# Four y tiles, gathers behind scatters, weight splits behind the expert's tiles, and an even pace for the next route

## The chip, the cores and the metric

The kernel runs on one core of a Trainium2 chip. The metric is the device time of one execution in microseconds, lower is better. Five engines work side by side, each through its own instructions in order: TensorE (PE, with its weight loads as PEld), VectorE (DVE), ScalarE (ACT), GpSimd (POOL) and SyncE (SP). They wait for each other by semaphores.

## What is computed

The first part is an attention without softmax on 8 sequences of 2496 rows: `x = u * (relu(z zT / S)^2 v)`. The second part sends the 19968 rows of x through eight experts, 2496 rows each, chosen greedily:

```python
logits = x @ w_gate
order = np.argsort(-logits.flatten())
for idx in order:
    tok, e = (int(idx) // E, int(idx) % E)
    if assigned[tok] >= 0 or counts[e] >= cap:
        continue
    assigned[tok] = e
    counts[e] += 1
for e in range(E):
    mask = assigned == e
    h = np.maximum(x[mask] @ w1[e], 0.0)
    out[mask] = h @ w2[e]
```

## The kernel before

The attention takes the first 1503 us or so. `route(0)` then finds the first expert to be filled and its rows, with nothing else to do beside it. After that the experts follow each other, in the order in which they fill up.

An expert is 5 groups of rows (four of 512, one of 448) times 8 tiles of the hidden layer, so 40 steps (`PER`). The loop over n (L633) runs, in each step: `layer2` of step n (12 matmuls of 128x256 into the PSUM tiles y0 and y1, L545 to L547), the items of `todo` for n, `advance`, `layer1` of step n + 3 (6 matmuls into hp, L514 to L516, then hh by ScalarE L533 and hl by VectorE L534), and `advance` again. Every product is three matmuls, of high and low halves.

`todo` holds, for a group that begins at n0: `gather_x` at n0 - 12 (four indirect gathers on GpSimd into an xg tile, L446), `turn_x` at n0 - 6 and n0 - 5 (transposes on TensorE L499, xh on ScalarE, xl on VectorE), and `put_y` at n0 + 7 (two copies of y0 and y1 to a y tile by ScalarE L572, four indirect scatters by GpSimd L578). `split_w` turns a weight block into two halves, by ScalarE (L473, w1h and w2h) and VectorE (L475, w1l and w2l). For an expert that begins at step n0 it stands at n0 - 10 to n0 - 7 for the first half of the hidden layer (c = 0), at n0 - 4 to n0 - 1 for the second (c = 1).

`route(k + 1)` is a generator, worked off in pieces beside expert k by `advance`, twice a step (80 half steps). Each `yield` has a weight; the weights between two half steps must reach the half step's share of `YIELDS`, 88. A route closes the full expert, finds each row's best one again, then searches a threshold in two stages of several rounds. A round is: the mask (VectorE, L299), a histogram of it (TensorE, L230, 10 matmuls), hd, hr and hx (VectorE, L234 to L237), the sum over partitions by `onesr` (TensorE, L317), best, Dg and T (VectorE). At the end stand a count (fmask, L347), a prefix sum (`tri`, L382), and the list of the expert's rows: 156 matmuls in four parts (L431), each behind four tiles' quarters of ob on VectorE (L425), which gives idx. The last route has no search.

The order of an engine's instructions is set by the scheduler, which takes the program's order and its own estimate of when an operand is ready. `tc.issue_after(x)` orders an instruction behind x on x's own engine, and adds no semaphore.

Of the kernel before, what the change touches and what calls it, by code (L numbers as in the profile page):

```python
# [8 lines left out]
F32 = mybir.dt.float32  # L9
# [4 lines left out]
AF = mybir.ActivationFunctionType  # L14
# [81 lines left out]
def moe(tc, xd, first, jp, identf, w1, w2, out, B, S, cp):  # L96
    nc = tc.nc
    E, D, F = w1.shape
# [4 lines left out]
    DH = D // 128  # L103
    FT = F // 128
    J = B * NT + B // 2
# [12 lines left out]
    AHEAD = 12  # L118
    YIELDS = 88
    with ExitStack() as ctx:  # L120
# [104 lines left out]
        def hist(masks, n, order):  # L225
            p = srch()
            per = NC // len(masks)
            for c in range(NC):
                q, r = divmod(c, per)
                nc.tensor.matmul(p[:, :n * 16], oh[:, c * 16:(c + 1) * 16].rearrange("p j e -> p (j e)"),  # L230
                                 masks[q](slice(r * 16, (r + 1) * 16)), start=(c == 0), stop=(c == NC - 1))
            v = p[:, :n * 16]
            v = v.rearrange("p (t j) -> p t j", t=n) if order == "tj" else v.rearrange("p (j t) -> p t j", t=n)
            nc.vector.tensor_mul(hd[:, :n, :16], v, diag[:, None, :].to_broadcast([128, n, 16]))  # L234
            r = rp.tile([128, ND], F32, name="hr")
            nc.vector.tensor_reduce(r[:, :n], hd[:, :n], axis=AX.X, op=OP.add)
            nc.vector.tensor_mul(hx[:, :, :n], r[:, None, :n].to_broadcast([128, E, n]),  # L237
                                 dE[:, :, None].to_broadcast([128, E, n]))
            return hx, n + n % 2

        paced = []

        def behind(lag):
            return tc.issue_after(paced[-lag].ins) if len(paced) >= lag else nullcontext()

        def route(k):
            if k:
                closed = rp.tile([128, E], F32, name="closed", tag="rab")
                nc.vector.tensor_scalar(closed, ROUTE[k - 1]["star"], SHUT, None, op0=OP.mult)
                for c in range(0, JP, JP // 2):  # L250
                    o = lg[:, c:c + JP // 2]
                    nc.vector.tensor_add(o, o, closed[:, None, :].to_broadcast([128, JP // 2, E]))
                    yield 0.7
                for c in range(0, JP, JP // 4):
                    eq = rp.tile([128, JP // 4, E], BF, name="eq")
                    best_expert(nc, rp, first, slice(c, c + JP // 4), eq)
                    yield 6.8 / 4
                done = rp.tile([128, JP], F32, name="done")
                nc.vector.tensor_scalar(done, asg, 0.0, GONE, op0=OP.is_gt, op1=OP.mult)
                nc.vector.tensor_add(m, m, done)  # L260
                order_keys(nc, first, slice(0, JP))
                yield 1.5
            last = k == E - 1
# [12 lines left out]
            else:  # L276
# [7 lines left out]
                for stage in range(2):  # L284
                    V = floor
                    for r, w in enumerate(widths):
# [7 lines left out]
                        for h in range(nh):  # L294
# [6 lines left out]
                            mask.append(lambda j, t=t, n=n: t[:, j, :n])  # L301
                        yield 2
                        x, nn = hist(mask, n, "jt")
# [6 lines left out]
                        elif r + 1 < len(widths):  # L310
                            W = rp.tile([128, ND], F32, name="W", bufs=2)
                            n2 = (1 << widths[r + 1]) - 1
                            nc.vector.tensor_tensor(W[:, :n2], step[:, r + 1, :n2], V.to_broadcast([128, n2]), op=OP.add)
                        yield 2.2
                        p = srch()
                        o = p[:, :E * nn]
                        nc.tensor.matmul(o, onesr, x[:, :, :nn], start=True, stop=True)  # L317
                        best = rp.tile([128, E, ND], F32, name="best")
# [8 lines left out]
                    if stage == 0:  # L327
                        base = rp.tile([128, 1], F32, name="base")
                        nc.vector.tensor_scalar(base, tstar, 65536.0, None, op0=OP.mult)
                        rel = rp.tile([128, JP], F32, name="rel")  # L330
                        nc.vector.scalar_tensor_tensor(rel, first["top"], base, first["low"],
                                                       op0=OP.subtract, op1=OP.add)
                        near = rp.tile([128, JP], I16, name="near")
                        nc.vector.tensor_scalar(near, rel, 32767.0, -32768.0, op0=OP.min, op1=OP.max)
                        spread(nc, xr, near)
                        yield 1.5
                T = tstar
# [3 lines left out]
                take()  # L341
                yield
                x, nn = hist([lambda j: g[:, :, j]], 2, "tj")
                yield
                p = srch()
                o = p[:, :E * 2]
                nc.tensor.matmul(o, onesr, x[:, :, :2], start=True, stop=True)  # L347
                o = o.rearrange("p (e t) -> p e t", t=2)
# [26 lines left out]
            if not last:  # L375
# [3 lines left out]
                nc.vector.scalar_tensor_tensor(rem, star, FULL, rem, op0=OP.mult, op1=OP.add)  # L379
            yield 2.5  # L380
            p = srch()
            nc.tensor.matmul(p[:, :nl], tri, tot[:, :nl], start=True, stop=True)  # L382
            off = rp.tile([128, 2], F32, name="off")
# [20 lines left out]
            yield 2  # L404
            idx = rp.tile([128, KT], I32, name="idx", bufs=2)
            ROUTE[k]["idx"] = idx
            obs = {}
            for a0, a1 in ((0, 4), (4, KT)) if k == 0 and KT > 4 else ((0, KT),):
                na = a1 - a0
                p = srch()  # L410
                for c in range(0, JP, CB):
# [5 lines left out]
                    for i, d in enumerate((idh, idl)):  # L417
                        nc.vector.tensor_mul(hl[:, :, i], oa, by_quad(d[:, q], na))
                    yield 1.5
                    if a0 == 0:  # L420
                        obs[c] = rp.tile([128, QN, 128, QW], BF, name="ob", bufs=4)
                        for b in range(0, 128, 32):
                            z = b + 32
                            with behind(4):
                                nc.vector.tensor_tensor(obs[c][:, :, b:z], by_quad(rab[:, 1, q], z - b),  # L425
                                                        slot[:, None, b:z].to_broadcast([128, QN, z - b, QW]),
                                                        op=OP.is_equal)
                            yield 1.5
                    for j in range(c, min(J, c + CB)):
                        n, r = divmod(j - c, QW)  # L430
                        nc.tensor.matmul(p[:, :2 * na], obs[c][:, n, :, r], hl[:, n, :, :, r],  # L431
                                         start=(j == 0), stop=(j == J - 1))
                    yield
                idl_f = rp.tile([128, KT], F32, name="idl_f")[:, :na]
# [24 lines left out]
        def split_w(k, layer, c, half):  # L459
# [13 lines left out]
            nc.scalar.activation(h, src, AF.Copy)  # L473
            if k:
                nc.vector.tensor_sub(l, src, h.bitcast(F32))  # L475
            else:
                with tc.issue_after(paced[-1].ins if paced else ROUTE[0]["listed"].ins):
                    nc.vector.tensor_sub(l, src, h.bitcast(F32))

        def gather_x(k, g):  # L480
            t = fp.tile([128, 4, D], F32, name="xg")
            idx = ROUTE[k]["idx"]
            for i in range(4):
                n = min(128, S - 512 * g - 128 * i)
                gather(t[:n, i], xd, idx[:n, 4 * g + i:4 * g + i + 1])
            XG[k, g] = t
# [23 lines left out]
        def expand(k, g, f, p, c):  # L510
            for d in range(DH):
                wh, wl = [t[:, d, f % 4] for t in W1[k, f // 4]]
                xh, xl = XH[k, g, d][:, c], XL[k, g, d][:, c]
                nc.tensor.matmul(p[:, c], wh, xh, start=(d == 0), stop=False)  # L514
                nc.tensor.matmul(p[:, c], wh, xl, start=False, stop=False)  # L515
                nc.tensor.matmul(p[:, c], wl, xh, start=False, stop=(d == DH - 1))  # L516

        def layer1(k, g, f):
# [13 lines left out]
            l = fp.tile([128, 512], F32R, name="hl_", bufs=LA + 1)[:, :w]  # L532
            nc.scalar.activation(h, p, AF.Relu)  # L533
            paced.append(nc.vector.scalar_tensor_tensor(l, p, 0.0, h.bitcast(F32), op0=OP.max, op1=OP.subtract))  # L534
            HH[k, g, f], HL[k, g, f] = h, l

        def contract(k, g, f, i):
# [8 lines left out]
            nc.tensor.matmul(o, h[:, c], wl, start=False, stop=False, skip_group_check=True)  # L546
            nc.tensor.matmul(o, l[:, c], wh, start=False, stop=final, skip_group_check=True)  # L547

# [12 lines left out]
        def put_y(k, g):  # L561
            y = fp.tile([128, 4, D], F32, name="y")
            idx = ROUTE[k]["idx"]
# [53 lines left out]
        def advance(pos):  # L617
# [4 lines left out]
            if pos < skip:  # L622
                return
            want = -(-(pos % (2 * PER) - skip + 1) * YIELDS // (2 * PER - skip))
            if (pos + 1) % (2 * PER) == 0:
# [339 lines left out]
```

## Time and profile before

| | |
|---|---|
| timed runs, us | 2693.76, 2694.63, 2691.26 |
| median, us | 2693.76 |
| profiled execution, us | 2689.33 |
| its span, us | 2687.6 |
| mean granted TensorE clock | 0.979 |
| attention, first route, experts | to about 1503, to about 1594, to the end |

A row of waits reads: engine, tile and line that waited, what it waited for, us in total, times, longest. A row of a timeline: start, duration, engine, line, operation, out<-in, with the idle time before it and what ended that. A row of windows: stretch, its length, then busy time and instructions of PE, PEld, DVE, ACT and POOL, the granted clock, the share and rate of the DMA engines. A row of groups: line, engine, operation, names, shapes, count, busy us, mean ns, idle time before. The wait rows of two stretches (1677 to 1745 us, 1745 to 2690 us) stand in one block in the prediction, apart by a line of dots.

### The profile page before, as it was taken

How to read it: one execution, taken by the hardware profiler on the slowest of the kernel's cores; microseconds unless marked ns; L12 is line 12 of the kernel's file. 1: busy time of each engine (PE TensorE's matmuls, PEld its weight loads, DVE VectorE, ACT ScalarE, POOL GpSimd, SP SyncE). 2: the span in 40 equal slices, each digit the busy share in tenths (PEclk: the TensorE clock that was granted, in tenths of full speed). 3: DMA queues.
4: the chain of work that ended last, by engine and by line, in shares of the span. 5: the costliest groups of instructions: out<-in, count | busy, mean ns of one | idle time of the engine just before them, and what ended most of it. 6: DMA issues, size and time to landing. Idle time of an engine off the chain costs nothing.

```text
span 2687.6 us, 51810 instructions
## 1 busy us (share of the span) xinstructions
PE 2584.4 (96%) x19733; PEld 2415.5 (90%) x19733; DVE 1968.6 (73%) x6093; ACT 1649.3 (61%) x2867; POOL 362.1 (13%) x506
## 2 busy tenths in 40 slices
PE   8999999999999999999999759899999999999998
PEld 8999999999999999999999647888989898889997
DVE  7788887787787887887877777868586868686322
ACT  8888888898888888888888312323333323333332
POOL 3000000000000000000000003232333323333331
PEclk9999999999999999999999769999999999999999
DMA  4121220121211211211100011111121211121110
GB/s 140 37 73 39 60 73 30 49 71 35 67 53 33 79 47 49 66 32 52 47 32 9 15 40 47 63 42 68 39 70 38 71 38 68 42 81 57 43 46 23
DMA packets 51210, 138.88 MB, mean 52 GB/s; under 512 B 10641, under 2 KB 18321, under 8 KB 50065
## 3 DMA queue, kind: packets, MB, share of 16 engines
q1 hardware_dynamic: 35856, 94.66, 11.3%
q0 software_dynamic: 15104, 40.91, 4.8%
q8 instruction: 154, 2.52, 0.4%
q14 instruction: 96, 0.78, 0.1%
HBM read 85.47 MB, written 40.89 MB: 47 GB/s over the span
## 4 chain that ended last, share of the span: by engine, by line
PE 93%; DVE 4%; another core or an unknown queue 1%; DMA 1%; issue 1%; ACT 1%; POOL 0%; POOLq 0%; ACTq 0%; SPq 0%
PE acc L804 14%; PE acc L801 14%; PE acc L803 13%; PE sc L761 7%; PE sc L760 7%; PE y L545 5%; PE hp L514 5%; PE y L547 5%; PE y L546 5%; PE hp L516 5%; PE hp L515 5%; PE srch L230 2%; PE srch L431 2%; PE xp L499 1%
## 5 line engine op out<-in xcount | busy, mean ns | idle before, releaser
L804 PE MATMUL acc<-vl,hi 128*128 128x256 f32 x3200 | 896.2, 282 | 0.0
L801 PE MATMUL acc<-vh,hi 128*128 128x256 f32 x3200 | 892.6, 281 | 0.0
L803 PE MATMUL acc<-vh,lo 128*128 128x256 f32 x3040 | 853.1, 281 | 0.6 <-DVE lo L785 0.6
L785 DVE TENSOR_TENSOR lo<-a,hi 128x512 fp32r<-128x512 f32 (+1 forms) x760 | 512.4, 674 | 221.9 <-ACT hi L774 203.9
L801 PEld LDWEIGHTS acc<-vh,hi 128*128 128x128 f32 x3200 | 601.3, 188 | 28.6
L804 PEld LDWEIGHTS acc<-vl,hi 128*128 128x128 f32 x3200 | 601.5, 188 | 1.6
L803 PEld LDWEIGHTS acc<-vh,lo 128*128 128x128 f32 x3040 | 570.9, 188 | 31.9 <-DVE lo L785 1.0
L763 ACT ACTIVATE r<-sc 128x512 f32<-128x512 f32 (+1 forms) x800 | 467.8, 585 | 140.6 <-PE sc L761 135.7
L533 ACT ACTIVATE hh<-hp 128x512 fp32r<-128x512 f32 (+1 forms) x320 | 187.5, 586 | 582.8 <-PE hp L516 432.0
L768 ACT ACTIVATE a<-r 128x512 f32<-128x512 f32 (+1 forms) x800 | 497.1, 621 | 24.9 <-DVE lo L785 0.4
L831 DVE SCALAR_TENSOR_TENSOR lt<-xs,wgb 128x256 bf16<-128x256 f32 x1248 | 472.2, 417 | 0.3
L545 PE MATMUL y<-w2h,hh 128*128 128x256 f32 (+1 forms) x1280 | 367.6, 287 | 17.2 <-ACT y L572 13.3
L546 PE MATMUL y<-w2l,hh 128*128 128x256 f32 (+1 forms) x1280 | 363.4, 284 | 0.0
L760 PE MATMUL sc<-za 128*128 128x512 f32 (+1 forms) x800 | 316.0, 395 | 0.0
L761 PE MATMUL sc<-zb,za 128*128 128x512 f32 (+1 forms) x800 | 312.8, 391 | 0.0
L774 ACT ACTIVATE hi<-a 128x512 fp32r<-128x512 f32 (+1 forms) x480 | 298.3, 622 | 14.6
L545 PEld LDWEIGHTS y<-w2h,hh 128*128 128x128 f32 (+1 forms) x1280 | 241.7, 189 | 28.6 <-ACT y L572 15.2
L514 PE MATMUL hp<-xh,w1h 128*128 128x512 f32 (+2 forms) x646 | 264.2, 410 | 0.3 <-ACT xh L507 0.3
L515 PE MATMUL hp<-xl,w1h 128*128 128x512 f32 (+2 forms) x646 | 252.3, 391 | 0.0
L546 PEld LDWEIGHTS y<-w2l,hh 128*128 128x128 f32 (+1 forms) x1280 | 241.6, 189 | 10.8 <-issue 1.6
L516 PE MATMUL hp<-xh,w1l 128*128 128x512 f32 (+2 forms) x646 | 251.3, 390 | 0.0
L578 POOL DMA_INDIRECT out_dram<-y,idx x160 | 179.6, 1123 | 402.9 <-ACT y L572 356.5
(1139 smaller groups left out, 3418.0 us busy)
## 6 DMA issues: line engine op xcount, KB each, us to landing
vr<-in_v_dram SPq DMA_DIRECT2D x32, 512.0 KB, 3.6
ur<-in_u_dram SPq DMA_DIRECT2D x32, 512.0 KB, 4.4
xd<-xs SPq DMA_DIRECT2D x32, 512.0 KB, 2.9
wr<-in_moe_w_dram SPq DMA_DIRECT2D x32, 512.0 KB, 4.4
zb<-za SPq DMA_DIRECT2D x14, 640.0 KB, 6.8
zin<-in_z_dram SPq DMA_DIRECT2D x32, 128.0 KB, 2.1
vr<-in_v_dram SPq DMA_DIRECT2D x8, 384.0 KB, 3.3
ur<-in_u_dram SPq DMA_DIRECT2D x8, 384.0 KB, 4.4
```

The lines of the kernel that those rows point to most:

```text
L514: nc.tensor.matmul(p[:, c], wh, xh, start=(d == 0), stop=False)
L545: nc.tensor.matmul(o, h[:, c], wh, start=first, stop=False, skip_group_check=True)
L546: nc.tensor.matmul(o, h[:, c], wl, start=False, stop=False, skip_group_check=True)
L760: nc.tensor.matmul(p, k, ZA[b][:, q], start=True, stop=False)
L761: nc.tensor.matmul(p, k, ZB[b][:, q], start=False, stop=True)
L763: nc.scalar.activation(r, p, AF.Relu, scale=scale)
L768: nc.scalar.activation(a, R.pop(n), AF.Square)
L785: nc.vector.tensor_sub(l, a, h.bitcast(F32))
L801: nc.tensor.matmul(o, h[:, c], vh, start=(kt == 0 and i % 2 == 0), stop=False, skip_group_check=True)
L803: nc.tensor.matmul(o, l[:, c], vh, start=False, stop=False, skip_group_check=True)
L804: nc.tensor.matmul(o, h[:, c], vl, start=False, stop=last, skip_group_check=True)
L831: nc.vector.scalar_tensor_tensor(t[r], XS[b, g][r, i], 1.0, WG["rows"][r, e], op0=OP.mult, op1=OP.mult, accum_out=lg[r, j, e:e + 1])
```

## The change

It has five parts.

- The y tile has four buffers, where it had the pool's two.
- `gather_x` orders its four gathers behind the last scatter written so far, on GpSimd.
- `split_w` of every expert but the first orders its ScalarE copy behind the last hh, and its VectorE subtraction behind the last hl.
- The search's and the list's matmuls (`in_turn`) stand on TensorE behind the last matmul of layer 1 or 2 written so far.
- The weights of the yields are new and sum to about 79 of 80 half steps in place of about 103 against a ceiling of 88, so that no remainder is left for the last half step.

```diff
+        halves = []
+        layered = []
+        def in_turn():
+            return tc.issue_after(layered[-1].ins) if layered else nullcontext()
...
 # in hist; the same with in_turn() at L317, L347, L382 and L431
-            for c in range(NC):
-                q, r = divmod(c, per)
-                nc.tensor.matmul(p[:, :n * 16], ...)
+            with in_turn():
+                for c in range(NC):
+                    q, r = divmod(c, per)
+                    nc.tensor.matmul(p[:, :n * 16], ...)
...
 # yields of a round, and of a part of the list
-                        yield 2
+                        yield 2 if n > 3 else 1.6
-                        yield 2.2
+                        yield 2
-                    yield 1.5
+                    yield 1
-                            yield 1.5
+                            yield 0.6
-                    yield
+                    yield 0.4
...
-            nc.scalar.activation(h, src, AF.Copy)
             if k:
-                nc.vector.tensor_sub(l, src, h.bitcast(F32))
+                with tc.issue_after(halves[-1].ins), tc.issue_after(paced[-1].ins):
+                    nc.scalar.activation(h, src, AF.Copy)
+                    nc.vector.tensor_sub(l, src, h.bitcast(F32))
...
-            for i in range(4):
-                n = min(128, S - 512 * g - 128 * i)
-                gather(t[:n, i], xd, idx[:n, 4 * g + i:4 * g + i + 1])
+            with tc.issue_after(scat[-1]) if scat else nullcontext():
+                for i in range(4):
+                    n = min(128, S - 512 * g - 128 * i)
+                    gather(t[:n, i], xd, idx[:n, 4 * g + i:4 * g + i + 1])
...
-                nc.tensor.matmul(p[:, c], wl, xh, start=False, stop=(d == DH - 1))
+                layered.append(nc.tensor.matmul(p[:, c], wl, xh, start=False, stop=(d == DH - 1)))
-            nc.scalar.activation(h, p, AF.Relu)
+            halves.append(nc.scalar.activation(h, p, AF.Relu))
-            nc.tensor.matmul(o, l[:, c], wh, start=False, stop=final, skip_group_check=True)
+            layered.append(nc.tensor.matmul(o, l[:, c], wh, start=False, stop=final, skip_group_check=True))
-            y = fp.tile([128, 4, D], F32, name="y")
+            y = fp.tile([128, 4, D], F32, name="y", bufs=4)
...
-            want = -(-(pos % (2 * PER) - skip + 1) * YIELDS // (2 * PER - skip))
+            want = (pos % (2 * PER) - skip + 1) * (2 * PER) / (2 * PER - skip)
```

The number of instructions is the same on every engine; their order differs. Three places show it. Lines of after are some 12 higher than those of before.

GpSimd, from the gathers of expert k's last group on to those of expert k + 1's first two groups (out_dram<-y is a scatter, xg<-xd,idx a gather, x8 that many in a row), before:

```order
L446 DMA xg<-xd,idx 128x256 x3
L446 DMA xg<-xd,idx 64x256
L578 DMA out_dram<-y,idx 19968x256 x8
L446 DMA xg<-xd,idx 128x256 x8
L578 DMA out_dram<-y,idx 19968x256 x4
L446 DMA xg<-xd,idx 128x256 x4
```

After:

```order
L455 DMA xg<-xd,idx 128x256 x3
L455 DMA xg<-xd,idx 64x256
L590 DMA out_dram<-y,idx 19968x256 x4
L455 DMA xg<-xd,idx 128x256 x4
L590 DMA out_dram<-y,idx 19968x256 x4
L455 DMA xg<-xd,idx 128x256 x4
```

The gathers of the two first groups no longer stand in one run of eight; four scatters stand between them, and so it stays to the end.

VectorE, one search round at the change from expert 2 to expert 3 (hl__28977 is the same tile in both), before:

```order
L319 SCALAR_TENSOR_TENSOR best<-srch,step_22638 128x8x7
L324 TENSOR_REDUCE Dg<-best 128x1
L292 TENSOR_TENSOR T<-W,Dg 128x7
L306 TENSOR_TENSOR V<-V,Dg 128x1
L299 TENSOR_TENSOR mask_28967<-rep,T 128x1120
L313 TENSOR_TENSOR W<-step_22638,V 128x7
L534 SCALAR_TENSOR_TENSOR hl__28977<-hp,hh 128x448
L234 TENSOR_TENSOR hd<-srch,diag 128x7x16
L236 TENSOR_REDUCE hr<-hd 128x7
```

After:

```order
L325 SCALAR_TENSOR_TENSOR best<-srch,step_22638 128x8x7
L330 TENSOR_REDUCE Dg<-best 128x1
L546 SCALAR_TENSOR_TENSOR hl__28935<-hp,hh 128x448
L297 TENSOR_TENSOR T<-W,Dg 128x7
L485 TENSOR_TENSOR w1l<-wr,w1h 128x512
L304 TENSOR_TENSOR mask_28946<-rep,T 128x1120
L311 TENSOR_TENSOR V<-V,Dg 128x1
L318 TENSOR_TENSOR W<-step_22638,V 128x7
L546 SCALAR_TENSOR_TENSOR hl__28977<-hp,hh 128x448
L234 TENSOR_TENSOR hd<-srch,diag 128x7x16
L485 TENSOR_TENSOR w1l<-wr,w1h 128x512
L236 TENSOR_REDUCE hr<-hd 128x7
```

Two halves of w1l now stand inside the round, one ahead of the mask and one ahead of hr, and an hl stands between best and T; the next round of after has the two halves of w2l at the same two places.

TensorE, the sum over partitions (onesr) that goes with this round's start, before:

```order
L546 MATMUL y_28770<-w2l,hh 64x256
L547 MATMUL y_28770<-w2h,hl__28842 64x256
L317 MATMUL srch<-hx,onesr 128x64
L514 MATMUL hp<-xh_28424,w1h 128x448
L515 MATMUL hp<-xl_28425,w1h 128x448
L516 MATMUL hp<-xh_28424,w1l 128x448
```

After:

```order
L527 MATMUL hp<-xl_28596,w1h 128x448
L528 MATMUL hp<-xh_28595,w1l 128x448
L323 MATMUL srch<-hx,onesr 128x64
L557 MATMUL y_28776<-w2h,hh 128x256
L558 MATMUL y_28776<-w2l,hh 128x256
L559 MATMUL y_28776<-w2h,hl__28842 128x256
```

It has moved from behind the layer-2 block that uses hl__28842 to ahead of it, right behind a layer-1 block, and the round's histogram has moved in the same way, ahead of the next layer-2 block.

More of the change, by code (lines that the diff above doesn't have):

```diff
@@ L118, in moe @@
     AHEAD = 12
-    YIELDS = 88
     with ExitStack() as ctx:
@@ L227, in hist @@
             per = NC // len(masks)
-            for c in range(NC):
-                q, r = divmod(c, per)
-                nc.tensor.matmul(p[:, :n * 16], oh[:, c * 16:(c + 1) * 16].rearrange("p j e -> p (j e)"),
-                                 masks[q](slice(r * 16, (r + 1) * 16)), start=(c == 0), stop=(c == NC - 1))
+            with in_turn():
+                for c in range(NC):
+                    q, r = divmod(c, per)
+                    nc.tensor.matmul(p[:, :n * 16], oh[:, c * 16:(c + 1) * 16].rearrange("p j e -> p (j e)"),
+                                     masks[q](slice(r * 16, (r + 1) * 16)), start=(c == 0), stop=(c == NC - 1))
             v = p[:, :n * 16]
@@ L252, in route @@
                     nc.vector.tensor_add(o, o, closed[:, None, :].to_broadcast([128, JP // 2, E]))
-                    yield 0.7
+                    yield 0.6
                 for c in range(0, JP, JP // 4):
@@ L256, in route @@
                     best_expert(nc, rp, first, slice(c, c + JP // 4), eq)
-                    yield 6.8 / 4
+                    yield 1.2
                 done = rp.tile([128, JP], F32, name="done")
@@ L261, in route @@
                 order_keys(nc, first, slice(0, JP))
-                yield 1.5
+                yield 1.4
             last = k == E - 1
@@ L313, in route @@
                             nc.vector.tensor_tensor(W[:, :n2], step[:, r + 1, :n2], V.to_broadcast([128, n2]), op=OP.add)
-                        yield 2.2
+                        yield 2
                         p = srch()
                         o = p[:, :E * nn]
-                        nc.tensor.matmul(o, onesr, x[:, :, :nn], start=True, stop=True)
+                        with in_turn():
+                            nc.tensor.matmul(o, onesr, x[:, :, :nn], start=True, stop=True)
                         best = rp.tile([128, E, ND], F32, name="best")
@@ L335, in route @@
                         spread(nc, xr, near)
-                        yield 1.5
+                        yield 1.2
                 T = tstar
@@ L341, in route @@
                 take()
-                yield
+                yield 2
                 x, nn = hist([lambda j: g[:, :, j]], 2, "tj")
-                yield
+                yield 2
                 p = srch()
                 o = p[:, :E * 2]
-                nc.tensor.matmul(o, onesr, x[:, :, :2], start=True, stop=True)
+                with in_turn():
+                    nc.tensor.matmul(o, onesr, x[:, :, :2], start=True, stop=True)
                 o = o.rearrange("p (e t) -> p e t", t=2)
@@ L379, in route @@
                 nc.vector.scalar_tensor_tensor(rem, star, FULL, rem, op0=OP.mult, op1=OP.add)
-            yield 2.5
+            yield 2.2
             p = srch()
-            nc.tensor.matmul(p[:, :nl], tri, tot[:, :nl], start=True, stop=True)
+            with in_turn():
+                nc.tensor.matmul(p[:, :nl], tri, tot[:, :nl], start=True, stop=True)
             off = rp.tile([128, 2], F32, name="off")
@@ L403, in route @@
                 nc.vector.scalar_tensor_tensor(asg, tm, cs, asg, op0=OP.mult, op1=OP.max)
-            yield 2
+            yield 1.6
             idx = rp.tile([128, KT], I32, name="idx", bufs=2)
@@ L418, in route @@
                         nc.vector.tensor_mul(hl[:, :, i], oa, by_quad(d[:, q], na))
-                    yield 1.5
+                    yield 1
                     if a0 == 0:
@@ L427, in route @@
                                                         op=OP.is_equal)
[L428 to L433, printed above, removed]
+                            yield 0.6
+                    with in_turn():
+                        for j in range(c, min(J, c + CB)):
+                            n, r = divmod(j - c, QW)
+                            nc.tensor.matmul(p[:, :2 * na], obs[c][:, n, :, r], hl[:, n, :, :, r],
+                                             start=(j == 0), stop=(j == J - 1))
+                    yield 0.4
                 idl_f = rp.tile([128, KT], F32, name="idl_f")[:, :na]
@@ L472, in split_w @@
                 h, l = [t[:, 2 * half:2 * half + 2] for t in W2[k, c]]
-            nc.scalar.activation(h, src, AF.Copy)
             if k:
-                nc.vector.tensor_sub(l, src, h.bitcast(F32))
+                with tc.issue_after(halves[-1].ins), tc.issue_after(paced[-1].ins):
+                    nc.scalar.activation(h, src, AF.Copy)
+                    nc.vector.tensor_sub(l, src, h.bitcast(F32))
             else:
+                nc.scalar.activation(h, src, AF.Copy)
                 with tc.issue_after(paced[-1].ins if paced else ROUTE[0]["listed"].ins):
```

## The prediction

> **What bounds the kernel now.** I read the page first, then the waits of TensorE after the attention, then the clock in short stretches, then the order of time at one expert's end.
>
> ```profile
> PE 2584.4 (96%) x19733; PEld 2415.5 (90%) x19733; DVE 1968.6 (73%) x6093; ACT 1649.3 (61%) x2867; POOL 362.1 (13%) x506
> PE   8999999999999999999999759899999999999998
> PEclk9999999999999999999999769999999999999999
> PE 93%; DVE 4%; another core or an unknown queue 1%; DMA 1%; issue 1%; ACT 1%; POOL 0%; POOLq 0%; ACTq 0%; SPq 0%
> ```
>
> TensorE is busy for 96% of the span and carries 93% of the chain that ended last. The number of its instructions does not change, so only three things can move the end: moments in which it stands still, moments at half clock, and new ones of either kind. The two dips (slices 23 to 25) are the first routing, which runs before any expert and keeps its order. The order of instructions differs from expert 0's 21st half-layer on, at about 1677 us. So I count TensorE's waits behind that point, in two stretches: 1677 to 1745 (the end of expert 0), then the rest.
>
> ```profile
> PE y L545 <- issue: 3.9, 3, 1.8
> PE srch L230 <- DVE mask L299: 3.3, 1, 3.3
> PE y L547 <- issue: 0.3, 1, 0.3
> ...
> PE y L545 <- ACT y L572: 13.3, 5, 2.7
> PE srch L317 <- DVE hx L237: 3.8, 4, 1.2
> PE srch L347 <- DVE hx L237: 1.6, 3, 0.5
> PE srch L347 <- PE hp L516: 0.5, 1, 0.5
> ```
>
> The first three rows are the first stretch: 3.9 + 3.3 + 0.3 = **7.5 us**. The others are the rest, in us, times and longest: **13.3 us** in five waits for the copy of a result (one at each later change of expert), and 3.8 + 1.6 + 0.5 = **5.9 us** for the search of the next route. Half clock comes on top:
>
> ```profile
> 1735.00:1745.00 10.00, 6.65 (x34) 6.12 (x32) 8.07 (x21) 3.88 (x7) 0.00 (x0) 0.50 0.00 0
> 2141.10:2147.90 6.80, 6.10 (x24) 5.84 (x25) 4.04 (x15) 3.45 (x6) 4.26 (x4) 0.50 0.19 66
> 2281.10:2284.50 3.40, 3.40 (x14) 3.14 (x13) 2.32 (x6) 1.03 (x2) 2.56 (x3) 0.50 0.22 77
> 2417.60:2421.00 3.40, 3.40 (x13) 3.14 (x12) 3.23 (x10) 1.08 (x2) 2.49 (x4) 0.50 0.25 82
> ```
>
> The second number is the stretch, then TensorE's busy time; the 0.50 is its granted clock. Work done at half clock would take half the time at full clock: (6.65 + 6.10 + 3.40 + 3.40) / 2 = **9.8 us**. All four stand right behind the change of an expert. All that the change could take away is so 7.5 + 13.3 + 5.9 + 9.8 = **36.5 us**, 1.4% of the span.
>
> **The gathers behind the scatters.** This is the largest term, and it rests on one reading: why does the copy of y come late? At the change from expert 1 to 2:
>
> ```profile
> 1863.97 0.36 PE L516 MATMUL hp<-xh,w1l 128*128 128x448 f32 x1
> 1864.02 0.99 POOL L446 DMA_INDIRECT xg<-xd,idx  x1 [0.30 <-issue]
> 1865.31 1.03 POOL L446 DMA_INDIRECT xg<-xd,idx  x1 [0.30 <-issue]
> 1866.65 0.95 POOL L446 DMA_INDIRECT xg<-xd,idx  x1 [0.30 <-issue]
> 1867.57 0.54 ACT L533 ACTIVATE hh<-hp 128x448 fp32r<-128x448 f32 x1 [5.30 <-PE hp L516]
> 1869.02 1.09 ACT L572 ACTIVATE y<-y 128x512 f32<-128x512 f32 x2 [0.91 <-remote]
> ...
> 2022.10 0.95 POOL L446 DMA_INDIRECT xg<-xd,idx  x1 [0.31 <-issue]
> 2022.36 0.36 PE L516 MATMUL hp<-xh,w1l 128*128 128x448 f32 x1
> 2022.77 0.54 ACT L533 ACTIVATE hh<-hp 128x448 fp32r<-128x448 f32 x1 [2.20 <-PE hp L516]
> ```
>
> The last matmul of a hidden tile ends at 1863.97 + 0.36 = 1864.33, and ScalarE, idle all the while, takes the tile at 1867.57: 3.2 us later, as the last of eight gathers in a row ends (1866.65 + 0.95 = 1867.60). Everything behind it on ScalarE (the copy of y at 1869.02 among it) is late by as much, and TensorE stands. The second piece is the same hand-over beside the last gathers of a run of four: the matmul starts at 2022.36, ScalarE at 2022.77, 0.41 us later and without loss. The rows around the other four waits read like the first piece; I found no such loss beside a run of four. The change lets no run of eight stand from expert 0's third group on. I therefore take all five waits away: **-13.3 us**. How a run of gathers could hold back a hand-over between two other engines the trace does not show, so that is a reading, and its failure is a rival. It costs nothing that I can see: the gathers that move back still have ten steps of some 2.8 us each before their transposes, and four take 4 x 1.3 = 5.2 us (1866.65 - 1865.31 is one).
>
> **Half clock.** Each of the four stretches follows such a standstill, so I take most of it away: **-8 us** of 9.8, since the new waits below may set off one again (bounds 0 and -9.8). The Trainium skill, "TensorE: Matmul & The Clock Gate", section "HAM oscillation — how this bites in real kernels", states that gaps in which the array idles over about 3.4 us bring the clock down. No wait here is that long (2.7 at most), and two of the five were followed by no half clock; by the page's words these waits are not its cause, and the 8 us would stay. This trace speaks for a looser condition, as all four stretches begin within a few us of a standstill; that the clock stays low is a rival below.
>
> ```profile
> L578 POOL DMA_INDIRECT out_dram<-y,idx x160 | 179.6, 1123 | 402.9 <-ACT y L572 356.5
> ```
>
> **Four y tiles.** A y tile's write waits for the four scatters of the tile two groups earlier. Two groups are 16 steps of about 2.8 us, some 45 us, while four scatters take 4 x 1.1 us on GpSimd, which mostly waits for y itself. I put it at 0 (bounds 0 and the five waits, which are counted already).
>
> **End of expert 0.** The 7.5 us come from a search that was handed to TensorE ahead of the mask it needs, and from late hand-overs in the same run of eight. The even pace puts this mask's matmuls a step later. I take **-5 us** (bounds 0 and -7.5), two thirds, since ScalarE's first split there also waits for a weight load that the change does not make earlier for certain.
>
> **The search, pinned and paced.** The old waits of 5.9 us go: **-5.9** (in the order of after, the w1l split no longer stands right ahead of that round). For what comes in their place, the row of a round at the change of expert 2 to 3, and what a split takes:
>
> ```profile
> 2021.24 0.19 PE L317 MATMUL srch<-hx,onesr 128*128 128x64 f32 x1
> 2021.47 0.22 DVE L319 SCALAR_TENSOR_TENSOR best<-srch,step 128x56 f32<-128x56 f32 x1
> 2021.97 0.17 DVE L292 TENSOR_TENSOR T<-W,Dg 128x7 int16<-128x7 f32 x1
> 2022.17 0.82 DVE L299 TENSOR_TENSOR mask<-rep,T 128x1120 bf16<-128x1120 int16 x1
> 2022.57 0.28 PE L545 MATMUL y<-w2h,hh 128*128 128x256 f32 x1
> 2023.34 0.62 DVE L534 SCALAR_TENSOR_TENSOR hl__28977<-hp,hh 128x448 fp32r<-128x448 f32 x1 [0.27 <-ACT hh L533]
> 2023.99 0.67 PE L230 MATMUL srch<-mask,oh 128*128 128x112 bf16 x10
> 2024.47 0.47 PE L514 MATMUL hp<-xh,w1h 128*128 128x512 f32 x1
> 2024.86 0.28 DVE L234 TENSOR_TENSOR hd<-srch,diag 128x112 f32<-128x112 f32 x1 [0.89 <-PE srch L230]
> ```
>
> ```profile
> L475 DVE TENSOR_TENSOR w1l<-wr,w1h 128x512 fp32r<-128x512 f32 x16 | 17.3, 1084 | 9.7 <-ACT w1h L473 8.3 <-issue 1.4
> L475 DVE TENSOR_TENSOR w2l<-wr,w2h 128x512 fp32r<-128x512 f32 x16 | 11.1, 693 | 2.6 <-ACT w2h L473 2.6
> L473 ACT ACTIVATE w1h<-wr 128x512 fp32r<-128x512 f32 x16 | 17.9, 1142 | 11.5 <-PE hp L515 6.9 <-DMA wr<-in_moe_w_dram 3.4 <-issue 1.3
> L425 DVE TENSOR_TENSOR ob<-rab,slot 128x1280 bf16<-128x1280 bf16 x64 | 50.1, 813 | 0.0
> L236 DVE TENSOR_REDUCE hr<-hd 128x7 f32<-128x119 f32 x32 | 8.9, 277 | 1.1
> L237 DVE TENSOR_TENSOR hx<-hr,dE 128x56 fp32r<-128x56 f32 x32 | 6.9, 217 | 1.1
> ```
>
> A layer-1 block takes TensorE 2022.57 - 2021.27 = 1.30 us (its first matmul starts 0.03 behind the row of 2021.24), a layer-2 block 2023.99 - 2022.57 = 1.42, a histogram 2024.47 - 2023.99 = 0.48. The new order is: layer 1, the sum of the histogram (onesr), layer 2, layer 1, histogram, layer 2, and so on. Counted from the sum's start, the next histogram is due at 1.42 + 1.30 = 2.72. Ahead of it VectorE must end hl, which it does 2023.96 - 2022.57 = 1.39 after a layer-1 block; then T (0.1 to the next start) and the mask (0.82): 2.3, so 0.4 is left. Counted from the histogram's start, the next sum is due at 0.48 + 2.72 = 3.20, and hd, hr and hx end at 1.39 + 0.28 + 0.28 + 0.22 = 2.2: 1.0 is left. So each round fits, and I put the pinning alone at 0.
>
> The splits of an expert's second half now stand inside these rounds, one in each of four. ScalarE's part is ordered behind hh, which ends at 0.20 + 0.55 = 0.75 (2022.77 against 2022.57), so w1h ends at 1.89 and w1l at 2.97. With w1l ahead of the mask, the mask ends at 3.79: 1.07 late. With w1l ahead of hr, hx ends at 2.97 + 0.50 = 3.47: 0.27 late. With w2l ahead of the mask: 1.5 + 0.69 + 0.82 = 3.0, 0.3 late. With w2l ahead of hr: 2.85, not late. Together 1.64, and with some 0.1 for each hand-over about **2.0 us** an expert. A next route with rounds runs beside these splits at five changes of expert: **+10 us**. The bounds are 0 and all four splits in full, 5 x 2 x (1.084 + 0.693) = 17.8.
>
> For the list of tokens the trace of before shows hardly a wait, because its matmuls could slide behind others; pinned, the first of a list can wait for one ob (0.813), and a w1h ahead of a copy of y holds that for up to 1.142. Bounds 0 and 6 x (0.813 + 1.142) = 11.7 for the six later lists; I take the middle, **+6 us**. The weight splits that leave the list phase give VectorE 2 x (1.084 + 0.693) = 3.6 us there, which is why I don't take more.
>
> **Sum.** -13.3 - 8 - 5 - 5.9 + 10 + 6 = -16.2 us. The profiled execution took 2689.3 us (span 2687.6 and 1.7 around it), so 2673.1. The median of the timed runs is 2693.76, 4.4 above it, so the forecast is **2677.5 us**.
>
> **The rivals.** (a) *The splits and the list hide.* For it: VectorE is at 73%, and my 0.3 to 1.1 us are differences of hand-overs. Against it: the w1h is in ScalarE's order behind hh, whatever the pace. Nothing is added and all 36.5 go: 2689.3 - 36.5 + 4.4 = 2657.
>
> (b) *The hand-over stays late.* For it: no row names the gathers as what ScalarE waits for. Against it: the end of the last gather and the release agree within 0.03 us. Then only 5 + 5.9 are won and 16 paid: 2689.3 + 5.1 + 4.4 = 2699.
>
> (c) *Slower: the pinned matmuls wait for VectorE in nearly every round.* The place is TensorE, which does its work in order: a histogram whose mask is late now holds the layer-2 block behind it, where before a block stood between. My slack for a mask is 0.4 us. There are 60 masks (12 for each of five experts). Once they are late by 0.15 us on average, 60 x 0.15 = 9 us go beside the 7.8 by which the splits can exceed my 10, and the gain is gone. At 0.3 us late each and splits in full: 2677.5 + 18 + 7.8 = 2703. For it: in the row of 2023.34, hl starts at once when hh ends, and every mask stands behind an hl. Against it: the 0.4 is from this trace's own hand-overs.
>
> (d) *The clock stays low where it was*, by causes other than the standstills: 8 us less, 2685.5.
>
> **Chances.** Forecast 0.50, (a) 0.15, (b) 0.12, (c) 0.15, (d) 0.08. The range leaves out part of (a) and (c): 2656 to 2702. A measurement of this kernel can tell about 0.2%, 5.4 us, from no change: faster means under 2688.4, slower over 2699.1. The forecast lies 16 us under, so of its 0.50 I give 0.42 to faster, 0.05 to no change, 0.03 to slower; (a) is faster; (d) is 0.05 faster, 0.03 the same; (b) lies on the upper bound, half and half; (c) is 0.12 slower, 0.03 the same. Sums: 0.62, 0.17, 0.21.
>
> **What would show it.** The row of the wait for the copy of y (13.3) should fall under 3, and no ScalarE row at a change of expert should start 3 us behind its matmul. The four half-clock stretches should be down to one or none. The wait of the histogram for its mask should show about ten times some 0.3 to 1.1 us, at w1l and w2l, and the wait of the list for ob about six times. If the first stays at 13, (b) is right; if the mask's wait has dozens of entries, (c) is; if neither appears and the time is under 2665, (a).

## The result and the profile after

| | before | after |
|---|---|---|
| median, us | 2694.2 | 2769.82 |
| lowest and highest, us | 2691.26 to 2696.52 | 2768.66 to 2772.12 |
| profiled execution and its span, us | 2689.33, 2687.6 | 2769.52, 2767.8 |

The changed kernel is slower: the ratio is 1.0279, with a 95% interval of 1.0266 to 1.0291. That is 75.6 us, and outside the range of the prediction. The page of after, its busy line and the shares of its chain:

```profile
PE 2605.5 (94%) x19733; PEld 2427.0 (88%) x19733; DVE 1962.5 (71%) x6093; ACT 1646.3 (59%) x2867; POOL 353.6 (13%) x506
...
PE 87%; DVE 7%; another core or an unknown queue 2%; issue 1%; ACT 1%; DMA 1%; POOL 0%; POOLq 0%; ACTq 0%
```

TensorE's part of the chain fell from 93% to 87%, VectorE's rose from 4% to 7%: TensorE waits. Its waits from 1745 to 2690 us (total, times, longest):

```profile
PE srch L230 <- DVE mask L304: 43.4, 19, 4.1
PE srch L390 <- DVE tot L377: 21.7, 5, 4.4
PE xp L511 <- DVE xl L520: 12.8, 10, 2.5
PE srch L390 <- DVE w2l L485: 1.4, 1, 1.4
```

The wait for the copy of y (13.3) is gone, as forecast. In its place stand waits of up to 4.4 us for VectorE, 79 us together. The forecast had about ten entries of the first kind, of 1.1 at most. Why is VectorE so late? One place in the timeline of after:

```profile
2063.41 0.90 POOL L590 DMA_INDIRECT out_dram<-y,idx  x1 [0.30 <-issue]
2064.62 0.99 POOL L455 DMA_INDIRECT xg<-xd,idx  x1 [0.30 <-issue]
...
2066.42 0.39 PE L528 MATMUL hp<-xh,w1l 128*128 128x512 f32 x1
2066.65 0.18 PE L323 MATMUL srch<-hx,onesr 128*128 128x32 f32 x1
2068.44 0.95 POOL L455 DMA_INDIRECT xg<-xd,idx  x1 [0.30 <-issue]
2071.03 0.60 ACT L545 ACTIVATE hh<-hp 128x512 fp32r<-128x512 f32 x1 [6.75 <-remote]
2071.06 0.18 DVE L325 SCALAR_TENSOR_TENSOR best<-srch,step 128x24 f32<-128x24 f32 x1 [4.64 <-remote]
2072.80 0.58 PE L230 MATMUL srch<-mask,oh 128*128 128x48 bf16 x10 [4.00 <-DVE mask L304]
```

GpSimd starts the last of four scatters at 2063.41 and, 0.30 us after it ends, the first of four gathers: eight indirect DMAs in a row. TensorE ends its hidden tile at 2066.81 and the sum over partitions at 2066.83. ScalarE and VectorE, both idle, take them at 2071.03 and 2071.06, over 4 us late and at the same moment. Only then best, T and the mask can follow, and TensorE stands 4.00 us at the histogram. This looks like the loss that the prediction had read at changes of expert, now inside the groups as well. One detail differs: the release comes 1.6 us after the last gather has ended (2068.44 + 0.95 = 2069.39), not with it. The stretch of 673 us from 1745 to 2418, of before and of after:

```profile
1745.00:2418.00 673.00, 653.61 (x5235) 592.65 (x5235) 490.41 (x1324) 208.70 (x349) 212.92 (x198) 0.99 0.17 56
```

```profile
1745.00:2418.00 673.00, 609.17 (x4702) 545.78 (x4702) 431.46 (x1185) 188.35 (x317) 181.37 (x176) 0.96 0.14 47
```

TensorE is busy 44 us less in the same time, and the granted clock falls to 0.96.

The two losses together account for the result. From 1677 us on, the rows of TensorE's waits add up to 27.1 us before and 85.7 after. At half clock TensorE is busy for 19.9 us before, in 4 stretches, and for 56.4 after, in 13, and half of that is lost. So 58.6 us came by waits and 18 by half clock, 77 us against 75.6 measured.

### The profile page after: what moved, and what is told of

It reads as the page before. It is cut to its first block, busy times and chain, and to the rows that moved or that the text cites. A ratio compares the mean times of both kernels' runs of the same rounds, so it can differ in the third digit from the quotient of the medians.

```text
span 2767.8 us, 51790 instructions
## 1 busy us (share of the span) xinstructions
PE 2605.5 (94%) x19733; PEld 2427.0 (88%) x19733; DVE 1962.5 (71%) x6093; ACT 1646.3 (59%) x2867; POOL 353.6 (13%) x506
## 4 chain that ended last, share of the span: by engine, by line
PE 87%; DVE 7%; another core or an unknown queue 2%; issue 1%; ACT 1%; DMA 1%; POOL 0%; POOLq 0%; ACTq 0%
PE acc L816 14%; PE acc L813 14%; PE acc L815 13%; PE sc L773 7%; PE sc L772 7%; PE hp L528 5%; PE hp L526 5%; PE y L557 5%; PE hp L527 5%; PE y L558 4%; PE y L559 4%; PE srch L230 2%; PE srch L440 2%; PE xp L511 1%
## 5 line engine op out<-in xcount | busy, mean ns | idle before, releaser
L557 PE MATMUL y<-w2h,hh 128*128 128x256 f32 (+1 forms) x1280 | 374.4, 293 | 0.0
```

What stands on the lines that cost most here:

```text
L557: nc.tensor.matmul(o, h[:, c], wh, start=first, stop=False, skip_group_check=True)
```

## The experiments

Every kernel was timed beside the kernel before. That kernel took about 2654 us in four sets of runs and about 2694 in two, as in the first measurement. I call the first condition prompt and the second late, for what the traces show. Ratios hold within a set only; intervals are 95%.

| run | condition, before | this, us | ratio |
|---|---|---|---|
| e1 changed, no gather order | prompt, 2653.9 | 2661.11 | 1.0027 (1.0017 to 1.0037) |
| e2 before, gather order alone | prompt | 2655.99 | 1.0006 (0.9997 to 1.0016) |
| e3 changed, no pinning | prompt | 2660.75 | 1.0025 (1.0015 to 1.0035) |
| e4 before, one xg tile | prompt | 2655.29 | 1.0004 (0.9994 to 1.0013) |
| a0 changed, again | prompt, 2653.8 | 2660.68 | 1.0026 (1.0016 to 1.0036) |
| e5 changed, one xg tile | prompt | 2662.12 | 1.0031 (1.0019 to 1.0044) |
| e8 changed, scatters held back | prompt | 2660.74 | 1.0026 (1.0016 to 1.0036) |
| e9 changed, splits free | prompt | 2668.27 | 1.0057 (1.0040 to 1.0073) |
| b0 before, again | late, 2693.8 | 2690.28 | one run |
| e10 changed, one xg tile, splits moved | late | 2666.30 | 0.9901 (0.9883 to 0.9918) |
| f1 to f4 = e2, e4, e1, e3 | prompt, 2653.8 | 2655.68, 2655.66, 2660.21, 2660.44 | 1.0006, 1.0006, 1.0024, 1.0025 |
| g1 = e2, gather order alone | late, 2694.1 | 2725.19 | 1.0114 (1.0097 to 1.0131) |
| g2 = e1, no gather order | late | 2680.66 | 0.9948 (0.9931 to 0.9964) |
| h1 = e3, h2 = e4 | prompt, 2654.3 | 2660.42, 2655.47 | 1.0024, 1.0003 |

**The first four: the gather order, the pinning, one xg tile.**

```diff
 # e1: the changed kernel with
-            with tc.issue_after(scat[-1]) if scat else nullcontext():
 # e2: the kernel before with that line added
 # e3: the changed kernel with
-            return tc.issue_after(layered[-1].ins) if layered else nullcontext()
+            return nullcontext()
 # e4: the kernel before with
-            t = fp.tile([128, 4, D], F32, name="xg")
+            t = fp.tile([128, 4, D], F32, name="xg", bufs=1)
```

> The changed kernel without the order of the gathers behind the scatters; its four y tiles, pinned search, splits and pace stay. Theory A (in the changed kernel the four gathers start right behind the four scatters, eight indirect DMAs in a row at every group, and for as long as they run TensorE's hand-overs to ScalarE and VectorE come 3 to 5 us late): the runs of eight are back to one a change of expert, so most of the 75 us goes: 2685 to 2710. Theory B (the pinned search and list wait for VectorE by themselves): hardly a change, 2755 to 2775.

> The kernel before with the order of the gathers behind the scatters alone. A: five runs of eight for each expert, so well slower than before, 2735 to 2770, with ScalarE's hh 3 us and more behind its matmul once in every group. B: 2690 to 2700, since nothing of the search is pinned.

> The changed kernel without the pinning of the search's and the list's matmuls; the gathers stay behind the scatters. A: the late hand-overs stay, but a late search no longer stops the layers' matmuls: 2725 to 2765. B: back to 2685 to 2700.

> The kernel before with one xg tile in place of two, so that the four gathers of a group wait for the transposes of the group ahead, some 11 us behind the last scatter and as far ahead of the next. A: no eight in a row anywhere, the five waits for the copy of y (13.3 us) and the half clock behind them (up to 9.8) go: 2665 to 2680. Theory C (the order scatter, gather, scatter, gather in itself brings the late hand-overs, whatever lies between them): as slow as e2. Theory D (two xg tiles are needed to hide the gathers): slower than 2700 by waits of xp for xg.

None of the theories foresaw this: the kernel before was 40 us faster, the single parts lay within 0.3% of it, and e2, with its runs of eight, cost nothing. So either the parts only hurt together, or the first measurement had something that these did not.

**The changed kernel again, and longer runs.** e5 is the changed kernel with one xg tile, e8 holds the scatters of every other group back, and e9 frees the splits:

```diff
 # e8
+            held.append((g, y, idx))
+            if (k * NG + g) % 2 == 0 and (k, g) != (E - 1, NG - 1):
+                return
+            for g, y, idx in held:
...
 # e9
-                with tc.issue_after(halves[-1].ins), tc.issue_after(paced[-1].ins):
+                if True:
```

> The changed kernel itself, on the chip of the experiments, where the kernel before takes 2654 and neither of the runs so far shows a late hand-over beside eight indirect DMAs in a row. Theory A2 (75 us come from hand-overs that come late beside runs of eight, and that is a condition of the chip or the session of the first measurement, not of the program alone): 2655 to 2670, no hand-over 3 us late, and the mask's wait near the 9.9 us of the run without the gather edge. Theory B (the parts together wait for each other, whatever the chip): 2715 and more, in the ratio of 1.028.

> The changed kernel with one xg tile, so that the gathers wait for the transposes of the group ahead and no eight stand in a row. A2: where hand-overs come late (before at 2694): under 2700; where they don't (before at 2654): as the changed kernel, within 5 us. B: as the changed kernel in both.

> The changed kernel with the scatters of every other group held until the next group's, so that eight scatters and up to eight gathers stand in a row. A2 with a threshold that depends on the length: late hand-overs appear here even where a run of eight brings none, 2690 and more. A2 without such a threshold on this chip: as the changed kernel, within 10 us.

> The changed kernel with the weight splits free again, as in the kernel before (gather edge, pinning and pace stay). If the splits that stand inside the rounds cost what the run without the gather edge shows (mask's wait 9.9 us, 10 times): about 10 us below the changed kernel on the same chip, at the kernel before or 2 to 5 us under it. If the pace costs it: no change.

a0 decides between them: the same program that took 2769.8 takes 2660.7, a ratio of 1.0026 to the kernel before. The same place of its timeline as above (the step of hl__29191):

```profile
2019.10 0.99 POOL L455 DMA_INDIRECT xg<-xd,idx  x1 [0.30 <-issue]
...
2020.89 0.39 PE L528 MATMUL hp<-xh,w1l 128*128 128x512 f32 x1
2021.12 0.18 PE L323 MATMUL srch<-hx,onesr 128*128 128x32 f32 x1
2021.31 0.60 ACT L545 ACTIVATE hh<-hp 128x512 fp32r<-128x512 f32 x1 [2.56 <-PE srch L323]
2021.35 0.18 DVE L325 SCALAR_TENSOR_TENSOR best<-srch,step 128x24 f32<-128x24 f32 x1 [1.54 <-PE srch L323]
...
2023.09 0.42 PE L230 MATMUL srch<-mask,oh 128*128 128x48 bf16 x10
```

Here too the gathers run right behind the scatters, and yet the tile that ends at 2021.28 is taken at 2021.31. The histogram does not wait. e8 did not do what it was made for: the first four of eight scatters had their y long before the last four, and the gathers waited for transposes, so its trace has 17 runs of eight and only one each of twelve and sixteen. Nothing is late in it, but it says nothing on the length of a run. What stays of TensorE's waits in a0, from 1677 us on, is mostly the search, where the splits now stand:

```profile
PE srch L230 <- DVE mask L304: 9.8, 10, 1.3
PE srch L390 <- DVE tot L377: 1.5, 2, 1.3
```

My expectation for e9 failed, and in its sign: freed splits cost 7.6 us more (2668.27 against 2660.68). Its waits in the same stretch tell why:

```profile
PE srch L440 <- DVE ob L433: 6.7, 6, 1.6
PE srch L230 <- DVE mask L304: 3.6, 5, 1.6
PE srch L323 <- DVE hx L237: 2.5, 4, 0.6
```

The mask's wait falls by 6.2 us as I expected, but the splits go back beside the list, whose matmuls now wait 6.7 us for ob, six times, and hx is late again. The order of the splits is thus what keeps the list free.

e3 does not test what it was made for. In its trace TensorE's 19733 matmuls stand in the same order, tile by tile, as in a0 and in after, so the line that pins them moved none of them. The search's new places, which the section on the change shows, come from the other parts of the change, and e3, like f4 and h1 with the same edit, is the changed kernel once more.

**A set in the late condition.** e10 is e5 with the second half's splits at every other step:

```diff
-                at(n0 - 4 + h if k else -1, split_w, k, 1, 1, h)
-                at(n0 - 2 + h if k else h, split_w, k, 2, 1, h)
+                at(n0 - 3 + 2 * h if k else -1, split_w, k, 1, 1, h)
+                at(n0 + 1 + 2 * h if k else h, split_w, k, 2, 1, h)
```

> The kernel before, for its profile on a chip of the experiments. Theory A2 (hand-overs come late beside eight indirect DMAs in a row on the first chip only): the five waits for the copy of y (13.3 us) and the half clock at changes of expert are absent, the wait of onesr for hx (3.8 to 4.8) is there, 2654. If the chip is like the first: 2694 and the waits as they were. Theory E (the first chip was slower in the attention too, by a clock or a memory): the 40 us are spread over the span.

> The changed kernel with one xg tile, and the second half's four weight splits at every other step, so that each stands behind hd and none ahead of a mask (slack 1.0 us there against 0.4). By the slack: the mask's wait of 9.8 falls under 3, so 5 to 8 us below the changed kernel on the same chip, at the kernel before or up to 4 us under it (2650 to 2656 where before takes 2654; under 2690 where before takes 2694, since no eight stand in a row). If the cost of the splits were their work and not their place: no change.

b0 shows the first measurement's picture again, here from 1593 us on: the wait for the copy of y is there, and hand-overs at changes of expert are late.

```profile
PE y L545 <- ACT y L572: 10.6, 4, 2.7
PE srch L230 <- DVE mask L299: 6.9, 3, 4.1
```

e10, in which no eight indirect DMAs stand in a row from the third group on, takes 2666.30, 1.0% less than the kernel before. It is the fastest kernel that ran in this condition. From 1677 us on its mask's wait is 6.3 us in five times, where a0 has 9.8 in ten; I had expected under 3. The prompt e5, which is e10 without the moved splits, has 9.8 too, but in another condition, so what the moved splits are worth stays open; e10 did not run in the prompt condition.

**The parts once more.** The next four, f1 to f4, were the same kernels as e2, e4, e1 and e3, meant for the late condition; they met the prompt one and only repeat the first set.

> The kernel before with the gathers ordered behind the scatters, alone, once more, for a chip on which before takes 2694 (late hand-overs). Theory A3 (75 us are hand-overs late beside runs of eight, five an expert by this order): 2735 to 2770 there. Rival (late hand-overs harm only with the pinned search): 2695 to 2705. Where before takes 2654: 2656 again.

> The kernel before with one xg tile, no eight in a row, for a chip on which before takes 2694. A3: 2655 to 2670. Rival (the 40 us between the two conditions are not those runs): 2690 and more. Where before takes 2654: 2655 again.

> The changed kernel without the gather order, for a chip on which before takes 2694. A3: one run of eight a change of expert as before, plus the 7 us of splits: 2690 to 2710. Rival (pinning makes each late hand-over cost far more): 2720 and more. Where before takes 2654: 2661 again.

> The changed kernel without the pinning, gather order kept, for a chip on which before takes 2694. A3: the late hand-overs stay; the layers themselves wait for hh, so 2740 to 2770. Rival (the pinned search turns them into time): under 2715. Where before takes 2654: 2661 again.

Then two of them met the late one:

> As f1, the gather order alone on the kernel before: 2735 to 2770 where before takes 2694 (A3), 2695 to 2705 if late hand-overs harm only with the pinned search; 2656 where before takes 2654.

> As f3, the changed kernel without the gather order: 2690 to 2710 where before takes 2694 (A3), 2720 and more if the pinning makes each late hand-over cost far more; 2661 where before takes 2654.

This separates the change. The gather order alone costs 31 us (2725.19 against 2694.07). The changed kernel without it is 13.4 us faster than before (2680.66), where with it, in the first measurement, it was 75.6 us slower. TensorE's matmuls stand in g1 in the order of before, and in g2 in that of after, so on TensorE the gather order moved nothing. TensorE's waits from 1677 us on, of g1 and then of g2:

```profile
PE srch L230 <- DVE mask L299: 18.2, 11, 3.8
PE xp L500 <- DVE xl L509: 10.0, 11, 1.5
PE srch L317 <- DVE hx L237: 7.3, 4, 3.5
```

```profile
PE srch L230 <- DVE mask L304: 9.2, 9, 1.6
PE y L556 <- ACT y L583: 6.2, 5, 1.3
PE y L556 <- issue: 2.9, 2, 2.6
```

Both lie under what was expected, g1 by 10 us, g2 by 9. And g1 has a place that reads like the one of after, at the eighth of a run. The tile of the matmul at 2049.15 is done at 2049.54 and is taken 4.3 us later:

```profile
2049.15 0.39 PE L517 MATMUL hp<-xh,w1l 128*128 128x512 f32 x1
...
2051.17 0.95 POOL L446 DMA_INDIRECT xg<-xd,idx  x1 [0.30 <-issue]
...
2053.80 0.60 ACT L534 ACTIVATE hh<-hp 128x512 fp32r<-128x512 f32 x1 [6.79 <-PE hp L517]
```

The last two runs were to tell why the gather order costs 31 us alone and 89 with the rest (2769.8 less 2680.7), and what before is without its runs of eight. They met the prompt condition:

> The changed kernel without the pinning, gather order kept. Where before takes 2694: 2700 to 2730 if the pinned search and list turn the late hand-overs of the runs of eight into most of the 89 us between the changed kernel (2770) and the one without the gather order (2681); 2750 to 2770 if the pinning plays no part. Where before takes 2654: 2661.

> The kernel before with one xg tile, no eight in a row. Where before takes 2694: 2655 to 2672 if the runs of eight make the 40 us between the two conditions; 2690 and more if not. Where before takes 2654: 2655.

Both repeat their earlier times, and these two questions stay open. h1 could not have answered the first, since its matmuls stand as in after.

**A count over all traces.** I took the moments at which TensorE's semaphore was raised, from 1677 us on, and searched each run of indirect DMAs for a pause of over 3.2 us (2.9 is usual in a0). In after, 29 of the 29 runs of four scatters and four gathers have one; in g1 26 of 29; in before and in g2 all five runs of eight gathers; in a0, prompt, 2 of 29. Runs of four often have one too in the late condition (before: 21 of 37 runs of scatters, 10 of 23 of gathers; g2: 35 of 37 and 14 of 23). So it is not a property of the number eight. That a run of four, some 5 us long, is mostly covered by the hh tiles that lie ready, and a run of eight, about 10 us, is not, is a reading that fits these counts; no run tests it.

The lateness itself can be measured as the time from the end of a matmul that raises the semaphore to the next moment at which it rises. For matmuls that end within a run of indirect DMAs, or up to 1 us behind it, it is over 1 us this often:

| trace, late condition | over 1 us | longest, us |
|---|---|---|
| before | 63 of 262 | 6.0 |
| after | 224 of 364 | 7.4 |
| g1 | 204 of 381 | 7.9 |
| g2 | 65 of 223 | 4.4 |
| e10 | 37 of 232 | 5.6 |

For all other matmuls of these traces it is never over 0.6 us, and in the 14 prompt traces it is never over 0.02 us, beside indirect DMAs or not. The semaphores of ScalarE and VectorE are late at such places too (over 1 us in before: 37 of 244 and 54 of 635; in a0 none). So the engine that takes a result is not slow; what it waits for rises late.

## Why the prediction was wrong

**The step that failed** is "The gathers behind the scatters", in its sentence "The change lets no run of eight stand from expert 0's third group on". The order of GpSimd's rows did change as shown, scatter x4, gather x4 and so on, but I took rows of four for runs of four. What parted them in time before was not the order. It was a wait, which GpSimd's waits of before from 1677 us on show, and those of after no longer:

```profile
POOL xg L446 <- PE xp L499: 153.4, 18, 14.0
```

```profile
POOL xg L455 <- issue: 94.5, 138, 10.8
POOL xg L455 <- PE hp L528: 18.8, 2, 18.5
```

Before, a group's gathers stood ahead of the scatters of a later group, and waited there for the transposes that freed their xg tile: 18 waits of 8.5 us on average, a pause in about half of the groups; other gaps stand under other names (PE srch L317: 41.7, 5, 8.3 is one). Behind a later scatter that tile is long free, so they start 0.30 us after it. In g1 this wait is gone as well, and in g2 it is back (18 waits, 140.1 us). The change turned five runs of eight into 29. So the term of -13.3 us had the place of the loss right and came out with the opposite sign: in the late condition the gather order costs 31 us alone and 89 in the changed kernel.

A second sentence failed with it, "I found no such loss beside a run of four". It may hold for TensorE's time, but the hand-overs are late there too: in the trace of before 38 of the 224 rises beside runs of four are over 1 us late.

**The mechanism.** That hand-overs come late beside long runs of indirect DMAs was "a reading". It is now shown, as something that holds in one condition: TensorE's semaphore rises over 1 us late beside indirect DMAs and nowhere else, the same program takes 2769.8 late and 2660.7 prompt, and the order alone costs 31 us. What brings a chip into the late condition, and how the DMAs hold the semaphores back, the runs do not show; the experiments changed neither. The agreement of 0.03 us between a release and the end of the last gather, which the prediction held against (b), did not repeat: it is 1.6 us in after.

**Half clock** (-8): right in size. It costs 9.9 us before and 1.7 in g2. There the longest wait for the copy of y fell from 2.7 to 1.3 us, and the clock from 1745 to 2418 us rose from 0.99 to 1.00. One stretch of 3.4 us is left, before 1745:

```profile
1745.00:2418.00 673.00, 656.97 (x5281) 591.32 (x5280) 494.19 (x1343) 213.33 (x355) 206.30 (x200) 1.00 0.17 56
```

So the half clock went with the standstills, and rival (d) falls. In after, with standstills of 4 us, it came back (0.96). The Trainium skill, "TensorE: Matmul & The Clock Gate", section "HAM oscillation — how this bites in real kernels", states a limit of about 3.4 us for gaps in which TensorE idles. This kernel's traces show half clock behind shorter ones: in before behind three of the five waits of 2.6 to 2.7 us, and in e9 within 3 us of waits of 1.1 and 1.6 us.

**The end of expert 0** (-5): over-sized. The waits from 1677 to 1745 us fell from 7.5 to 4.5 us in g2, so by 3.

**The splits** (+10): about right in size. The mask's wait is 9.8 us in 10 times, longest 1.3, in a0; the forecast named "about ten times some 0.3 to 1.1". Freeing the splits takes 6.2 of the 9.8 away (e9).

**The list** (+6): mis-sized, it is 0. In a0 no wait of the list for ob is left, since the splits that left it are worth more there than I allowed: with them back, e9 pays 6.7 us.

**The search's old waits** (-5.9): the wait for hx is gone in a0 and g2. It is no matter of the late condition, for the prompt e4, with TensorE's order as before, has it:

```profile
PE srch L317 <- DVE hx L237: 4.8, 4, 1.2
```

So in the prompt condition the change takes this wait away and adds that of the mask, while no hand-over is late that it could repair. The waits are 11.3 us in a0 against 7.2 in e4, which makes 4 of a0's loss of 6.9 us.

**The pinning** (0): 0, but not because each round fits, as the prediction argued. It moves no matmul (e3 against a0), so it cannot be what makes 31 us into 89. g1 and after have nearly as many late rises (204 and 224), but TensorE's order differs, and in after 70 of the 85.7 us of waits are those of the next route's matmuls for mask, tot, hx and low. So that route's new order, which the other parts of the change bring, is the likely cause; no run shows it. **The four y tiles** (0) and the pace ran in no kernel by themselves.

**The sum.** Without its failed part the change does about what the forecast said: 2680.7 measured in g2, 2677.5 forecast. That is partly chance: five runs of eight gathers stay in g2, whose waits fell from 13.3 to 6.2 and not to 0, and the list's 6 us did not come. **The rivals**: (b), the hand-over that stays late, came nearest in kind, but I gave it 2699, since it let the runs be and did not multiply them. (c) named the right place, TensorE at the histogram behind a late mask, and the wrong cause.

## What to carry to other kernels

An order edge moves an instruction in a queue, but not in time: ask which wait kept two bursts apart before, and whether it still stands between them after. Here, one xg tile keeps scatters and gathers apart by a real wait; the changed kernel with that, and moved splits, was the fastest in the late condition (2666.3). An order edge can also move nothing: compare the order of instructions with and without it before it is given a price. Where a kernel's time differs by 40 us between sets of runs, repeat the changed kernel itself beside its parts before any part is blamed.

## What the hardware showed that I had not expected

The same program differs by 1.5% before the change (2654 and 2694) and by 4% after it (2661 and 2770) between two conditions that hold for a whole set of runs. They differ in how soon an engine's semaphore rises while indirect DMAs run: ScalarE takes its tile 0.03 us after the matmul's end at 2021.31 in a0, and 4.2 us after it at 2071.03 in after. Chips of other sets did not settle it: one chip number showed both conditions.
